# A spectral-mixing and SwiGLU kernel on one core: first batch's filter products, filter loads, weight loads and first normalisations rearranged

## The chip, the core and the metric

The kernel runs on one core of one Trainium2 chip. The metric is the device time in microseconds (us), taken as the median of 17 runs of the same program. The core has five engines that each work through their own instruction stream in order: TensorE (PE in the profile, with its weight loads as PEld), VectorE (DVE), ScalarE (ACT), GpSimd (POOL) and SyncE (SP). DMAs are issued from SP and ACT (hardware queues) and from POOL (the software queue). All matmul results land in PSUM, which GpSimd does not read in this kernel: what it multiplies is first copied out of PSUM by ScalarE.

## The reference

```python
def _attn_ref(x, filt_r, filt_i):          # x: 8 x 3008 x 256, filters: 1505 x 256
    X = np.fft.rfft(x, axis=1)
    F = (filt_r + 1j * filt_i)[None, :, :]
    return np.fft.irfft(X * F, n=x.shape[1], axis=1)

def _moe_ref(x, w_gate, w_val, w_out, rms_g):   # x: 24064 x 256, d_ff 1536
    rms = np.sqrt(np.mean(x * x, axis=-1, keepdims=True) + 1e-06)
    xn = x / rms * rms_g
    g = xn @ w_gate
    silu = g * (1.0 / (1.0 + np.exp(-g)))
    val = xn @ w_val
    return silu * val @ w_out
```

The first function filters every batch along the sequence in the frequency domain; its output, as 24,064 tokens of width 256, goes through an RMS norm and a gated feed-forward layer.

## The kernel before

**The Fourier transform** of length 3008 is split as 47 x 64. For each of the 8 batches there are these steps, and each has a small function that issues its instructions:

- `x_load(b, c)`, c = 0 to 3: the input, cast to fp16 on the way in, by two DMAs of the software queue each (L175).
- `a_unit(b, i)`, i = 0 to 11: a matmul with the table `wa` over the 64-long axis, evicted by ScalarE (L191, L193). Three units fill a chunk, which `z_store(b, c)` writes to the scratch tensor `z_tmp` in DRAM by four DMAs of the SP queue (L201). This first bounce through DRAM turns the layout.
- `t2_load(b, c)`: one chunk of eight of the 32 frequencies k2, read back from `z_tmp` (L205). A chunk needs all the stores of its batch.
- `b_unit(b, i)`, i = 0 to 15: two k2 each. Two matmuls with the table `wb` over the 47-long axis (L212) give a 128 x 512 block `psb` in PSUM; its product with the filter's real part gives `s1` (L217), with the imaginary part `s2`. In the first batch, the second product of odd units is made by GpSimd from a copy `v` that ScalarE takes out of PSUM (L221, L222); all other products are VectorE's (L217, L224).
- `bi_unit(b, i)`: four matmuls with the inverse table `wi` on `s1` and `s2` (L232), evicted by ScalarE (L237). In the first batch it comes one unit behind `b_unit`. Two units fill a chunk, which `g_store` writes to `g_tmp` (L240), the second bounce.
- `t4_load(b, c)`: four DMAs that read `g_tmp` back (L249). In the first batch half of them are issued from ScalarE's queue and half from SP's.
- `n_unit(b, m, dh)`, m = 0 to 5: the inverse over the 64-long axis, giving a tile of 512 tokens, evicted once as `y` (with the norm's gain) and once squared (L264, L271, L273). `q_unit` sums the squares by matmuls with `ones` (L281) and takes the power -1/2 on GpSimd (`rho`, L293). `rho_move` stores rho to DRAM and reads it back broadcast to all partitions (L297, L299), and `xn_unit` multiplies on GpSimd (L339). For the first tile of all, `norm_first` spreads rho by matmuls with `ident` instead (`psr`, L324) and multiplies on VectorE (L328).

**The feed-forward layer** is a list of 8 x 6 x 12 = 576 items (b, m, jt). For item i the loop issues `gv` (four matmuls, a Silu on ScalarE and a product on VectorE: L359, L363, L364), then what `plan` has for slot i, then `down` of item i-2 (four matmuls, L376). The plan is written out by hand: `at(slot, fn, ...)` puts the transform of batch b+1 between the items of batch b.

**Before that loop** stands a preamble that does the whole transform of batch 0 with little beside it. It also loads the filters: `f_load(c)`, c = 0 to 3, six software DMAs (eight for c = 0), fills partitions 0 to 63 of chunk c of `fr` and `fi` after these have been set to zero by VectorE (L450, L451, L463, L464); `f_dup(c)` copies them to partitions 64 to 127, `fr` on VectorE (L417) and `fi` on ScalarE (L418). `wi_group(g)`, g = 0 to 7, makes the table `wi` by transposing `wb` (L425 to L429). `gate(ap)` is a one-element copy on GpSimd (L436): what is behind it in GpSimd's stream is not issued until `ap` is there. `w_load(q)` loads half of the three weight matrices by three software DMAs (L441, L442).

All streams are in the order in which the program issues them (`manual_schedule`). The order around the change is, in the preamble before:

```python
        gate(st[0]["t1"][3][0:1, 5, 0:1])
        f_load(1)
        wb_load(2)
        wb_load(3)
        for c in range(3):
            t2_load(0, c)
        gate(st[0]["t2"][0][0:1, 0, 0:1])
        f_load(2)
```

and, in the plan for batch 1, `a0, b0, bs = (6, 22, 7)`: `a_unit`s from slot 6 on, `z_store`s at slots 9, 12, 15 and 18, `t2_load`s from slot 19, `b_unit`s from slot 22, seven slots for four of them.

Of the kernel before, what the change touches and what calls it, by code (L numbers as in the profile page):

```python
# [35 lines left out]
KC = 8  # L36
# [66 lines left out]
def kernel(  # L103
# [104 lines left out]
    def b_unit(b, i):  # L208
        ps = bank(0 if b else i % 2, "psb").rearrange("p (a d) -> p a d", a=2)
        for u in range(2):  # L210
            k = 2 * i + u
            nc.tensor.matmul(ps[:, u, :], wb[:, k, :], st[b]["t2"][k // KC][:, k % KC, :],  # L212
                             start=True, stop=True)
        s1 = sp.tile([P, 2, D], FP16, tag="s1", name="s1")
        s2 = sp.tile([P, 2, D], FP16, tag="s2", name="s2")
        c, r = divmod(2 * i, KC)
        nc.vector.tensor_tensor(out=s1, in0=ps, in1=fr[c][:, r:r + 2, :], op=ALU.mult)  # L217
        if b == 0 and i % 2:
            v = yp.tile([P, 2, 512], FP32, tag="y", name="v")
            v = v[:, 0, :].rearrange("p (a d) -> p a d", a=2)  # L220
            nc.scalar.activation(out=v, in_=ps, func=AXT.Copy)  # L221
            nc.gpsimd.tensor_tensor(out=s2, in0=v, in1=fi[c][:, r:r + 2, :], op=ALU.mult)  # L222
        else:
            nc.vector.tensor_tensor(out=s2, in0=ps, in1=fi[c][:, r:r + 2, :], op=ALU.mult)  # L224
        st[b]["s"][i] = (s1, s2)
# [13 lines left out]
    def g_store(b, c):  # L239
        nc.sync.dma_start(g_d[b, 4 * c:4 * c + 4, :, :].rearrange("k p d -> p k d"),  # L240
                          st[b]["t3"].pop(c))

    def t4_load(b, c):
        t = t4p.tile([P, XC, D], FP16, tag="t4", name="t4")
        for h in range(2):
            for ri in range(2):
                p0 = h * 64 + ri * 32
                r0 = ri * SL + h * H + c * XC
                (nc.scalar if b == 0 and h else nc.sync).dma_start(t[p0:p0 + 32, :, :],  # L249
                                                                   g_d[b, :, r0:r0 + XC, :])  # L250
        st[b]["t4"][c] = t
# [51 lines left out]
    def norm_first():  # L303
# [11 lines left out]
        st[0]["sq"][0] = sq  # L315
        q_unit(0, 0)
        rho = st[0]["u"].pop(0)
# [3 lines left out]
        ps = bank(1, "psr")  # L321
# [7 lines left out]
        st[0]["xn"][0] = xn  # L329
# [103 lines left out]
    def gate(ap):  # L433

        g = up.tile([1, 1], FP32, tag="gate", name="gate")
        nc.gpsimd.tensor_copy(out=g, in_=ap)  # L436

    def w_load(q):
        cols = ts(q, DFF // 2)
        for src, dst in ((moe_w_gate, wg), (moe_w_val, wv)):  # L440
            nc.gpsimd.dma_start(dst[:, :, cols], src.rearrange("(dt p) j -> p dt j", p=P)[:, :, cols])  # L441
        nc.gpsimd.dma_start(wo[:, ts(q, JT // 2), :],  # L442
                            moe_w_out.rearrange("(jt p) d -> p jt d", p=P)[:, ts(q, JT // 2), :])

    def wb_load(c):
        nc.sync.dma_start(wb[:, c * KC:(c + 1) * KC, :], wb_d[:, c * KC:(c + 1) * KC, :])

    with tc.manual_schedule():
        nc.vector.memset(mhalf, -0.5)
        nc.vector.memset(fr[0][0:HALF], 0.0)  # L450
        nc.vector.memset(fi[0][0:HALF], 0.0)  # L451
# [4 lines left out]
        f_load(0)  # L456
# [3 lines left out]
        wb_load(1)  # L460
        for c in range(NC):
            if c:
                nc.vector.memset(fr[c][0:HALF], 0.0)  # L463
                nc.vector.memset(fi[c][0:HALF], 0.0)  # L464
            for i in range(3):
                a_unit(0, 3 * c + i)
            z_store(0, c)
        nc.vector.memset(ones, 1.0)
        gate(st[0]["t1"][3][0:1, 5, 0:1])
        f_load(1)  # L470
        wb_load(2)
        wb_load(3)
        for c in range(3):
            t2_load(0, c)
        gate(st[0]["t2"][0][0:1, 0, 0:1])
        f_load(2)
# [4 lines left out]
        for g in range(4):  # L481
            wi_group(g)
        f_dup(0)
        for g in range(4, 8):
            wi_group(g)
        for i in range(17):
            if i < 16:
                b_unit(0, i)
            if i == 1:
                f_load(3)  # L490
            if i == 7:
                w_load(0)
            if i == 11:
                w_load(1)
            if i == 15:
                for c in range(NXC):
                    x_load(1, c)
            if i % 4 == 1 and i // 4 + 1 < NC:
                f_dup(i // 4 + 1)
            if i >= 1:  # L500
                bi_unit(0, i - 1)
                if i % 2 == 0:
                    g_store(0, i // 2 - 1)
            if i == 4:
                t2_load(0, 3)
        for c in range(NXC):
            t4_load(0, c)
        norm_first()
        n_unit(0, 1, 0)
        n_unit(0, 1, 1)  # L510
        q_unit(0, 1)
        rho_move(0, 1)
# [82 lines left out]
```

## Time and profile before

| What | us |
|---|---|
| median of 17 runs | 1018.61 (1016.1 to 1021.99) |
| the profiled execution, its time | 1018.67 |
| the profiled execution, its span from first to last instruction | 1016.9 |
| PE busy in the span | 931.9 (92%) |
| first matmul of the first batch's `b_unit` (L212) | 32.52 |
| first matmul of `norm_first` (L310) | 85.24 |
| first matmul of `gv` (L359) | 95.02 |
| PE busy in the 817 us from 200 us on | 797.2 |

The time of a run is 1.8 us longer than the span of its profile. A row of the timeline is: start, duration, engine, line, operation, output <- input, and in brackets how long the engine sat idle before it and what ended that. A row of the chain is start, length and what was at work. A row of the windows is a stretch, its length, then the busy time of each engine with its number of instructions, the granted TensorE clock, the share of the DMA engines and GB/s.

### The profile page before, as it was taken

What the parts mean: (1) busy time and instruction counts of PE and PEld (TensorE: products, weight loads), DVE (VectorE), ACT (ScalarE), POOL (GpSimd) and SP (SyncE); (2) the same over time, 40 slices, a digit from 0 to 9 for tenths busy, and PEclk for the clock granted to TensorE, in tenths of its full rate; (3) what the DMA queues carried; (4) which work ended last, traced back from release to release, by engine and by line L of the source; (5) the groups of instructions that cost most, each with busy time, mean ns of one, the idle gap of its engine ahead of it and who ended that gap; (6) DMA issues with size and microseconds to landing.
All of it is one profiled execution on the core that took longest, in us unless ns stands there. A gap on an engine that the chain in (4) does not pass through costs nothing.

```text
span 1016.9 us, 17359 instructions
## 1 busy us (share of the span) xinstructions
PE 931.9 (92%) x6279; PEld 570.0 (56%) x6279; DVE 601.0 (59%) x980; ACT 602.7 (59%) x1060; POOL 249.2 (25%) x221
## 2 busy tenths in 40 slices
PE   2444989999999999999999999999999999999997
PEld 1222556655665566655665566655665556656554
DVE  8532467645774477645775468644775467645554
ACT  4442755666655765567655765567656766566543
POOL 5460341032311232032411323031410322023200
PEclk9999999999999999999999999999999999999999
DMA  9994373435723374324724365324734353312211
GB/s 193 158 172 110 79 176 77 105 76 134 150 63 105 93 162 112 99 70 123 153 60 123 86 146 126 106 50 113 160 83 123 86 121 89 100 51 61 43 42 39
DMA packets 94565, 107.25 MB, mean 105 GB/s; under 512 B 17224, under 2 KB 69064, under 8 KB 94288
## 3 DMA queue, kind: packets, MB, share of 16 engines
q1 hardware_dynamic: 85104, 87.59, 33.3%
q0 software_dynamic: 8992, 17.77, 11.9%
q8 instruction: 49, 0.80, 0.3%
q10 hardware_dynamic: 384, 0.79, 0.3%
q14 instruction: 36, 0.29, 0.1%
HBM read 70.88 MB, written 49.90 MB: 119 GB/s over the span
## 4 chain that ended last, share of the span: by engine, by line
PE 75%; DMA 9%; ACT 5%; issue 4%; DVE 3%; POOL 2%; SPq 1%; ACTq 0%; DVEq 0%; POOLq 0%
PE po L376 22%; PE pg L359 21%; PE pv L359 20%; PE psi L232 5%; PE psb L212 3%; DMA z_tmp<-t 3%; DMA t<-z_tmp 3%; PE psn L264 2%; DMA fi<-in_filt_i_dram 2%; ACT t L193 1%; ACT sq L273 1%; SPq L201 1%; PE psa L191 1%; DVE s L217 1%; DMA g_tmp<-t 1%
## 5 line engine op out<-in xcount | busy, mean ns | idle before, releaser
L364 DVE TENSOR_TENSOR hh<-pv,sg 128x512 f16<-128x512 f32 (+1 forms) x576 | 390.8, 679 | 349.5 <-ACT sg L363 224.9
L363 ACT ACTIVATE sg<-pg 128x512 f16<-128x512 f32 (+1 forms) x576 | 340.6, 591 | 309.1 <-PE pg L359 306.7
L376 PE MATMUL po<-wo,hh 128*128 128x256 f16 (+1 forms) x2304 | 361.2, 274 | 3.1 <-DVE o L383 0.9
L359 PE MATMUL pg<-xn,wg 128*128 128x512 f16 (+1 forms) x1152 | 340.0, 377 | 0.0
L359 PE MATMUL pv<-xn,wv 128*128 128x512 f16 (+1 forms) x1152 | 338.8, 376 | 0.0
L376 PEld LDWEIGHTS <-hh 128*128 128x128 f16 (+1 forms) x2304 | 221.5, 98 | 110.7 <-issue 33.3
L339 POOL TENSOR_TENSOR xn<-y,rb 128x1024 f16<-128x1024 f32 (+1 forms) x47 | 129.6, 2758 | 310.9 <-DMA rb<-r_tmp 234.5
L359 PEld LDWEIGHTS <-wv 128*128 128x128 f16 x1152 | 113.1, 98 | 132.1 <-issue 2.1
L293 POOL TENSOR_TENSOR rho<-u,mhalf 128x4 f32<-128x4 f32 x48 | 48.7, 1015 | 367.3 <-DVE u L291 354.0
L359 PEld LDWEIGHTS <-wg 128*128 128x128 f16 x1152 | 105.6, 98 | 21.6
L232 PE MATMUL psi<-s,wi 128*128 128x256 f16 x512 | 85.4, 290 | 19.7 <-POOL s L222 13.1
L217 DVE TENSOR_TENSOR s<-psb,fr 128x512 f16<-128x512 f32 x128 | 87.3, 682 | 21.5 <-PE psb L212 21.4
L237 ACT ACTIVATE t<-psi 96x512 f16<-96x512 f32 x128 | 75.9, 593 | 38.7 <-PE psi L232 38.4
L232 PEld LDWEIGHTS <-wi 128*128 128x128 f16 x512 | 51.9, 103 | 54.3 <-issue 15.3
L224 DVE TENSOR_TENSOR s<-psb,fi 128x512 f16<-128x512 f32 x120 | 81.6, 680 | 0.0
L271 ACT ACTIVATE y<-psn,gsb 128x512 f32<-128x512 f32 (+1 forms) x94 | 64.4, 685 | 10.4 <-PE psn L264 5.3
L212 PE MATMUL psb<-t,wb 96*128 96x256 f16 x256 | 53.1, 292 | 14.3 <-DMA t<-z_tmp 13.7
L193 ACT ACTIVATE t<-psa 128x512 f16<-128x512 f32 x96 | 57.9, 612 | 11.9 <-PE psa L191 9.0
L273 ACT ACTIVATE sq<-psn 128x512 f16<-128x512 f32 (+1 forms) x94 | 55.6, 591 | 0.0
L191 PE MATMUL psa<-xc,wa 128*128 128x512 f16 x96 | 37.5, 408 | 10.8 <-DMA xc<-in_x_dram 9.5
L212 PEld LDWEIGHTS <-wb 96*128 96x128 f16 x256 | 24.9, 104 | 37.4 <-issue 16.3
L264 PEld LDWEIGHTS <-t 128*128 128x128 f16 x376 | 29.6, 100 | 21.6 <-issue 1.1
(52 smaller groups left out, 287.4 us busy)
## 6 DMA issues: line engine op xcount, KB each, us to landing
out_dram<-o SPq DMA_DIRECT2D x88, 256.0 KB, 3.7
z_tmp<-t SPq DMA_DIRECT2D x128, 96.0 KB, 2.2
t<-z_tmp SPq DMA_DIRECT2D x32, 384.0 KB, 6.0
g_tmp<-t SPq DMA_DIRECT2D x64, 192.0 KB, 2.5
rb<-r_tmp SPq DMA_DIRECT2D x47, 256.0 KB, 4.2
t<-g_tmp SPq DMA_DIRECT2D x120, 96.0 KB, 2.5
xc<-in_x_dram POOLq DMA_DIRECT2D x56, 192.0 KB, 6.2
out_dram<-o SPq DMA_DIRECT2D x8, 192.0 KB, 3.0
```

The source lines that it names most:

```text
L193: nc.scalar.activation(out=dst, in_=src, func=AXT.Copy)
L212: nc.tensor.matmul(ps[:, u, :], wb[:, k, :], st[b]["t2"][k // KC][:, k % KC, :], start=True, stop=True)
L217: nc.vector.tensor_tensor(out=s1, in0=ps, in1=fr[c][:, r:r + 2, :], op=ALU.mult)
L224: nc.vector.tensor_tensor(out=s2, in0=ps, in1=fi[c][:, r:r + 2, :], op=ALU.mult)
L232: nc.tensor.matmul(ps[:, u, :], wi[:, 2 * i + u, q, :], s12[q][:, u, :], start=(q == 0), stop=(q == 1))
L237: nc.scalar.activation(out=st[b]["t3"][c][:, 2 * r:2 * r + 2, :], in_=ps[0:KR], func=AXT.Copy)
L273: nc.scalar.activation(out=st[b]["sq"][m][:, dh, 0:w], in_=ps[:, 0:w], func=AXT.Square)
L339: nc.gpsimd.tensor_tensor(out=xv[:, :, 0:nq], in0=yv[:, :, 0:nq], in1=rv[:, 0:nq].unsqueeze(1).to_broadcast([P, 2, nq, P]), op=ALU.mult)
L359: nc.tensor.matmul(ps[:, 0:w], wt[:, dt_, ts(jt, P)], xn[:, dt_, 0:w], start=(dt_ == 0), stop=(dt_ == 1))
L363: nc.scalar.activation(out=sg[:, 0:w], in_=pg[:, 0:w], func=AXT.Silu)
L364: nc.vector.tensor_tensor(out=hh[:, 0:w], in0=pv[:, 0:w], in1=sg[:, 0:w], op=ALU.mult)
L376: nc.tensor.matmul(po[s4 // 2][0:w, s4 % 2, :], hh[:, s4 * P:s4 * P + w], wo[:, jt, :], start=(jt == 0 and s4 % 2 == 0), stop=(jt == JT - ...
```

## The change

The diff, cut to its core:

```diff
@@ b_unit
-        s1 = sp.tile([P, 2, D], FP16, tag="s1", name="s1")
-        s2 = sp.tile([P, 2, D], FP16, tag="s2", name="s2")
         c, r = divmod(2 * i, KC)
-        nc.vector.tensor_tensor(out=s1, in0=ps, in1=fr[c][:, r:r + 2, :], op=ALU.mult)
-        if b == 0 and i % 2:
+        f1, f2 = fr[c][:, r:r + 2, :], fi[c][:, r:r + 2, :]
+        if b:
+            s1 = sp.tile([P, 2, D], FP16, tag="s1", name="s1")
+            s2 = sp.tile([P, 2, D], FP16, tag="s2", name="s2")
+        else:
+            s1, s2 = (hp.tile([P, 512], FP16, tag=g, name=g).rearrange("p (a d) -> p a d", a=2)
+                      for g in ("sg", "hh"))
+        eng = nc.vector
+        if b == 0 and i % 2 and i > 4:
+            eng = nc.gpsimd
             v = yp.tile([P, 2, 512], FP32, tag="y", name="v")
             v = v[:, 0, :].rearrange("p (a d) -> p a d", a=2)
             nc.scalar.activation(out=v, in_=ps, func=AXT.Copy)
-            nc.gpsimd.tensor_tensor(out=s2, in0=v, in1=fi[c][:, r:r + 2, :], op=ALU.mult)
-        else:
-            nc.vector.tensor_tensor(out=s2, in0=ps, in1=fi[c][:, r:r + 2, :], op=ALU.mult)
+            ps = v
+        eng.tensor_tensor(out=s1, in0=ps, in1=f1, op=ALU.mult)
+        eng.tensor_tensor(out=s2, in0=ps, in1=f2, op=ALU.mult)
@@ t4_load
-                (nc.scalar if b == 0 and h else nc.sync).dma_start(t[p0:p0 + 32, :, :],
+                (nc.scalar if b == 0 and c == 0 and h else nc.sync).dma_start(t[p0:p0 + 32, :, :],
@@ norm_first, cut in two helpers that also take tile 1
+        scale_split(0)
+        scale_apply(0, 1)
+    def scale_split(m):
+        rho = st[0]["u"].pop(m)
         hl = up.tile([P, 2, 4], FP16, tag="hl", name="hl")
         nc.vector.tensor_copy(out=hl[:, 0, :], in_=rho)
         nc.vector.tensor_tensor(out=hl[:, 1, :], in0=rho, in1=hl[:, 0, :], op=ALU.subtract)
+    def scale_apply(m, bk):
+        ps = bank(bk, "psr")
...
@@ w_load: thirds in place of halves
-        cols = ts(q, DFF // 2)
+        cols = ts(q, DFF // 3)
...
@@ preamble
         for c in range(NXC):
             x_load(0, c)
-        f_load(0)
...
         for c in range(NC):
-            if c:
-                nc.vector.memset(fr[c][0:HALF], 0.0)
-                nc.vector.memset(fi[c][0:HALF], 0.0)
+            for t in (fr[c], fi[c]):
+                if c < 2 or (c == 2 and t is fr[c]):
+                    nc.vector.memset(t[0:HALF], 0.0)
+                else:
+                    nc.scalar.activation(out=t[0:HALF].rearrange("p a d -> p (a d)"),
+                                         in_=mhalf[0:HALF, 0:1].to_broadcast([HALF, KC * D]),
+                                         func=AXT.Copy, scale=0.0)
+        nc.vector.memset(ones, 1.0)
+        f_load(0)
+        for c in range(NC):
             for i in range(3):
                 a_unit(0, 3 * c + i)
             z_store(0, c)
-        nc.vector.memset(ones, 1.0)
-        gate(st[0]["t1"][3][0:1, 5, 0:1])
-        f_load(1)
-        wb_load(2)
-        wb_load(3)
+            if c == 1:
+                wb_load(2)
+                wb_load(3)
+                wi_group(0)
+                wi_group(1)
         for c in range(3):
             t2_load(0, c)
         gate(st[0]["t2"][0][0:1, 0, 0:1])
+        f_load(1)
         f_load(2)
...
-        for g in range(4):
+        for g in range(2, 8):
             wi_group(g)
         f_dup(0)
-        for g in range(4, 8):
-            wi_group(g)
-        for i in range(17):
+        for i in range(19):
             if i < 16:
                 b_unit(0, i)
-            if i == 1:
+            if i == 5:
+                t2_load(0, 3)
                 f_load(3)
-            if i == 7:
+            if i == 9:
                 w_load(0)
-            if i == 11:
-                w_load(1)
-            if i == 15:
-                for c in range(NXC):
-                    x_load(1, c)
-            if i % 4 == 1 and i // 4 + 1 < NC:
+            if i % 4 == 2 and i // 4 + 1 < NC:
                 f_dup(i // 4 + 1)
-            if i >= 1:
-                bi_unit(0, i - 1)
+            if i >= 3:
+                bi_unit(0, i - 3)
                 if i % 2 == 0:
-                    g_store(0, i // 2 - 1)
-            if i == 4:
-                t2_load(0, 3)
+                    g_store(0, i // 2 - 2)
         for c in range(NXC):
             t4_load(0, c)
+        gate(st[0]["t4"][0][0:1, 0, 0:1])
+        w_load(1)
+        w_load(2)
         norm_first()
         n_unit(0, 1, 0)
         n_unit(0, 1, 1)
-        q_unit(0, 1)
-        rho_move(0, 1)
+        for c in range(NXC):
+            x_load(1, c)
@@ plan
-        at(4, xn_unit, 0, 1)
+        at(1, q_unit, 0, 1)
+        at(3, scale_split, 1)
+        at(5, scale_apply, 1, 0)
         for m in range(2, 6):
-            norm_plan(0, m, (m - 2) * 10)
+            norm_plan(0, m, 2 + (m - 2) * 9)
-            a0, b0, bs = (6, 22, 7) if b == 1 else (0, 16, 8)
+            a0, b0, bs = (8, 24, 6) if b == 1 else (0, 16, 8)
```

In the first batch both products of a unit are now on one engine: GpSimd's for units 5, 7, 9, 11, 13 and 15, VectorE's for the others, and `s1` and `s2` have four buffers in place of three. The inverse follows three units behind in place of one. Three of the eight zero fills go to ScalarE. The second half of the table `wb` is loaded between the second and third group of first-bounce stores on SP, and two groups of `wi` are made there; the filters' chunk 1 is issued behind the gate on the first `t2_load`, so that all filter chunks stay on the software queue. Of the weights, the first third is loaded during the filter products, the other two thirds and the input of batch 1 behind a new gate on the first `t4_load`. The second token tile of batch 0 takes the matmul way of `norm_first` in place of the DRAM way. The plan of batches 0 and 1 is shifted.

More of the change, by code (lines that the diff above doesn't have):

```diff
@@ L315, in norm_first @@
         st[0]["sq"][0] = sq
+        st[0]["y"][0] = y
         q_unit(0, 0)
-        rho = st[0]["u"].pop(0)
+        scale_split(0)
+        scale_apply(0, 1)
+    def scale_split(m):
+        rho = st[0]["u"].pop(m)
         hl = up.tile([P, 2, 4], FP16, tag="hl", name="hl")
@@ L320, in norm_first @@
         nc.vector.tensor_tensor(out=hl[:, 1, :], in0=rho, in1=hl[:, 0, :], op=ALU.subtract)
-        ps = bank(1, "psr")
+        st[0]["u"][m] = hl
+    def scale_apply(m, bk):
+        hl = st[0]["u"].pop(m)
+        y = st[0]["y"].pop(m)
+        ps = bank(bk, "psr")
         for q in range(4):
@@ L328, in norm_first @@
             nc.vector.tensor_tensor(out=xn[:, dh, :], in0=ps, in1=y[:, dh, :], op=ALU.mult)
-        st[0]["xn"][0] = xn
+        st[0]["xn"][m] = xn
     def xn_unit(b, m):
@@ L438, in w_load @@
     def w_load(q):
-        cols = ts(q, DFF // 2)
+        cols = ts(q, DFF // 3)
         for src, dst in ((moe_w_gate, wg), (moe_w_val, wv)):
             nc.gpsimd.dma_start(dst[:, :, cols], src.rearrange("(dt p) j -> p dt j", p=P)[:, :, cols])
-        nc.gpsimd.dma_start(wo[:, ts(q, JT // 2), :],
-                            moe_w_out.rearrange("(jt p) d -> p jt d", p=P)[:, ts(q, JT // 2), :])
+        nc.gpsimd.dma_start(wo[:, ts(q, JT // 3), :],
+                            moe_w_out.rearrange("(jt p) d -> p jt d", p=P)[:, ts(q, JT // 3), :])
     def wb_load(c):
@@ L449 @@
         nc.vector.memset(mhalf, -0.5)
-        nc.vector.memset(fr[0][0:HALF], 0.0)
-        nc.vector.memset(fi[0][0:HALF], 0.0)
         warm = up.tile([P, 4], FP32, tag="rho", name="warm")
```

## The prediction

> **What bounds the kernel now.** I read the page's slices first, then the engines' windows by stage.
>
> ```profile
> PE   2444989999999999999999999999999999999997
> DMA  9994373435723374324724365324734353312211
> PE 75%; DMA 9%; ACT 5%; issue 4%; DVE 3%; POOL 2%; SPq 1%; ACTq 0%; DVEq 0%; POOLq 0%
> ```
> ```profile
> 36.00:71.00 35.00, 21.02 (x92) 12.88 (x92) 19.07 (x27) 18.83 (x26) 20.18 (x23) 1.00 1.01 150
> 71.00:94.00 23.00, 3.90 (x34) 2.87 (x33) 3.10 (x7) 3.16 (x6) 4.81 (x9) 1.00 0.69 155
> 104.00:120.00 16.00, 15.99 (x108) 9.47 (x106) 7.89 (x13) 13.25 (x24) 6.74 (x4) 1.00 0.30 66
> 120.00:140.00 20.00, 16.10 (x104) 9.44 (x102) 9.08 (x16) 9.78 (x17) 5.37 (x5) 0.91 0.67 158
> 200.00:1017.00 817.00, 797.18 (x5446) 487.81 (x5443) 489.69 (x817) 502.18 (x892) 184.41 (x136) 1.00 0.41 98
> ```
>
> From 95 us on TensorE has 96 to 100% of nearly every window: that part is its work, which the change leaves alone but for eight small matmuls. Time can come only from the preamble, where no engine is full, and from the window 120 to 140. The chain of waits names the pieces, the timeline the stations:
>
> ```profile
> 34.71 8.12 DMA fi<-in_filt_i_dram
> 43.73 1.28 POOL s L222
> ...
> 71.82 9.82 DMA g_tmp<-t
> 81.91 2.59 DMA t<-g_tmp
> ...
> 130.51 3.93 DMA t<-z_tmp
> ```
> ```profile
> 28.52 1.48 SPq L205 DMA_DIRECT2D t<-z_tmp  x3
> 32.54 0.18 POOL L436 CAST gate<-t 1x1 f32<-1x1 f16 x1 [12.09 <-DMA t<-z_tmp]
> 35.58 0.69 DVE L217 TENSOR_TENSOR s<-psb,fr 128x512 f16<-128x512 f32 x1
> ...
> 69.06 1.26 POOL L222 TENSOR_TENSOR s<-v,fi 128x512 f16<-128x512 f32 x1 [3.09 <-ACT v L221]
> ...
> 89.56 1.04 POOL L293 TENSOR_TENSOR rho<-u,mhalf 128x4 f32<-128x4 f32 x1 [14.75 <-DVE u L291]
> ```
>
> Stations: first chunk back at 32.5, first product 35.6, last inverse evicted 71.8, its store landed 81.7, first matmul of norm_first 85.24, first gate matmul 95.02.
>
> **Start and bounce.** Three zero fills go to ScalarE, 3 x 1.91 (the row of the same 64x2048 shape, f_dup's fi) after the 2.23 at which it is free: done near 8.2, while its first eviction stands at 8.88. Hidden; without that cover up to 5.7. VectorE is free at 12 in place of 18. f_load(1), 752 KB, leaves the bounce; at the 195 to 240 GB/s of the windows there it took about 3.8. The floor is SP's own issue: the last z store left at 21.1, the inserted wb loads cost it about 1, and the fastest landing of these stores was 4.0. So the reads start near 25.2, not 28.5, and land near 29.0 (28.5 to 30.5): -3.5. For wi, TensorE waited 11.8 for wb until 28.64, and VectorE's last wi came 6.9 later. The wb loads, now ahead of the last eight stores, leave near 15 and land (4.8 to 7.0) by 22: wi done at 29, f_dup(0) 1.2 more. First product 30.2, before 35.58.
>
> **Filters.** Here the change takes back. f_load(1) stands where f_load(2) stood, behind the gate at 32.54. That one's fourth DMA landed at 42.83, gate + 10.3. So chunk 1 is whole at 29 + 11 = 40 for fi and 38 for fr. VectorE makes units 0 to 2 (six products 0.60 apart) by 33.8 and stands before f_dup(1) until 38. ScalarE's copy runs 40 to 42, and behind it in its stream wait two evictions and unit 5's copy v, 0.6 each. GpSimd multiplies unit 5 from 43.8 to 46.4.
>
> t2_load(0,3), now at unit 5 on SP, is wanted by unit 12: 0. GpSimd then issues f_load(3), which took 3.9 (39.79 to 43.73): 50.3. Chunk 2 follows chunk 1 on the queue at the 104 GB/s of the windows 36 to 46, 7.3: whole near 47.5. Chunk 3 lands 8.1 (fi's median) to 9 after issue, about 58.7; f_dup(3) to 60.6; the eviction and unit 11's v to 61.8.
>
> **Products.** Before, a pair of units took 4.2 (GpSimd starts at 60.67 and 64.71 for instance): one GpSimd product, then matmuls, eviction and VectorE in a ring, since the inverse followed one unit behind. Three behind opens the ring; a pair then costs what its busiest engine needs: GpSimd 2 x 1.27 = 2.54, VectorE 2 x 0.60 = 1.2, TensorE 12 x 0.213 = 2.6, ScalarE 1.8. [...] VectorE alone would need 4 x 0.60 = 2.4 a pair plus 1.2 per f_dup[...]. I keep 2.54. Units 11, 13, 15: 61.8 + 7.6 = 69.4, bound from below by GpSimd's own chain without the wait on chunk 3: 46.4 + 3.9 + 2.54 x 2 + 2.4 (weights) + 7.6 = 65.4. f_dup(2) and f_dup(3) lie beside GpSimd's products. [...] The row says 1.67 in place of 1.27 beside a copy: 2 x 0.4, mostly ahead of the wait on chunk 3. I take 0. From GpSimd's last end to the last store took 70.32 to 71.82, 1.5. The last g store leaves at 70.7 (67 to 73): -1.1.
>
> **Second bounce.** This is the largest term. That store took 9.82 while half of the weights (1.15 MB) and x(1) (1.54 MB) were on the DMA engines (windows 62 to 80: mostly 190 to 236 GB/s). Now only a third of the weights comes before it, issued near 56 and landed by 66; the rest waits behind the gate on t4. I price the store at the 2.5 of its row in the page, the read at 3.1 (page 2.5, second of two DMAs a queue 0.6): norm_first at 70.7 + 2.5 + 0.1 + 3.1 = 76.4, before 85.24: **-8.8**.
>
> **First normalisations.** Before, 9.78 to the first gate matmul. ScalarE issued eight DMAs until 87.3, so its square came 1.3 late; now it issues two. But behind the new gate GpSimd has, in this order, six weight DMAs (4.5 to 4.8), rho(0,0), the eight DMAs of x(1) and rho(0,1): rho(0,0) starts at +4.9, before at +4.3: 0.6 later. q_unit(0,1), which stood before gv and waited for ScalarE, goes to slot 1: -1.7. First gate matmul at +8.7: **-1.1**. Issuing x(1) behind it, GpSimd lets at most eight of its DMAs be open (the issue at 43.12 waited 0.56 for the one eight earlier), so the last x waits until the weights have landed, +13.5 (1.57 MB, and 1.18 MB of t4 reads, at about 210 GB/s), and rho(0,1) comes at +15; scale_split wants it in slot 3, +16.5. A cover of 1.5: cost 0 (0 to 3). jt 4 wants the second third at +16, landed near +9; slot 8 wants x at +20, landed at +16.
>
> **Loop.** Tile 1 gives up rho_move and xn_unit: two DMAs on SP and 2.86 of GpSimd, neither on TensorE's path: 0. psr for it: 8 matmuls of 128 columns, 0.43. Units of batch 1 every 1.5 slots in place of 1.75: window 140 to 160 lost 0.8 that way; I add 0.7 (0 to 1.5). The stall: SP stood behind rho_move(0,3) at slot 15 (its read waited 3.6 for the store), the last z stores left until 128.5, the read landed 3.93 later. TensorE then ran at half pace from 134.6 to 137.6, 1.5 more: 5.5 in all. Now rho_move is in slot 16 and b_unit in 24, eight slots apart, not seven, so the stores are bound by their own evictions as in later batches. Those waited 7.8 in six batches, 1.3 each, none over 1.9 and with no slow matmuls behind. I take 1.3: **-4.2** (-5.5 to 0).
>
> **Sum** against the profiled execution, 1018.67 (span 1016.9 and 1.8 outside): -8.8 - 1.1 + 0.4 + 0.7 - 4.2 = -13.0, so 1005.7. The median of the runs, 1018.61, stands at the same place; I say 1005.5.
>
> **Rivals.** *Filters come faster.* With chunk 1 alone behind the gate its landing needs less than 11, and GpSimd's chain decides: store at 66.9, 3.8 less: 1001.7. For it: units then wait for nothing else. Against it: the windows 36 to 46 show only about 104 GB/s with the DMA engines full.
> *The wait only moves.* Chunk 3 lands later, the store leaves at 73 (+2.3), and SP is again late in the loop, with the slow clock (+4.2): 1012.
> *Slower: GpSimd's stream at the gate.* Rho(0,0) is queued behind six weight DMAs of 1.57 MB, where three weight DMAs at most were seen open at once. If the queue can't hold them, GpSimd stands until they land: rho at +14 in place of +5, rho(0,1) behind x(1) at +24 or more with VectorE's products behind it, some 7 more. 9 + 7 = 16 against the 13.0 gained: 1018.7 + 3 = 1021.7. It decides once that wait passes 13. Against it: both w_loads were issued in 2.4 each without a wait.
> *It doesn't do what it says:* chunk 1 behind the gate costs the products what the bounce saves, and the last g store, still held by other traffic, lands at 81 as now; the loop gains nothing: 1017 to 1019.
>
> **How the numbers follow.** Forecast 0.57 (1002 to 1009), faster filters 0.17, the wait moved 0.19, GpSimd's stream 0.04, nothing 0.03. What can be told from no change is 0.2%, 2 us. Faster: 0.57 + 0.17 + 0.19 = 0.93; within: 0.03; slower: 0.04. The range takes both neighbours in, with 2.7 below the faster one for the lower ends of the DMA terms: 999 to 1012.5.
>
> **What would show it.** Right: first products near 30, VectorE idle until about 38 before f_dup(1), GpSimd with two 1.27 products a pair, g store landed within 3, norm_first near 76, gv near 85, psb's wait in batch 1 under 2 with no slow matmuls. Wrong: z stores still landing at 28, a long idle of GpSimd among the six weight issues, hl waiting for rho in slot 3, or g store still taking 8.

## The result and the profile after

| | before | after |
|---|---|---|
| median, us | 1018.81 (47 runs) | 1009.56 (1008.51 to 1010.24, 8 runs) |
| after / before | | 0.9907, interval 0.9895 to 0.9919 |
| span of the profiled execution | 1016.9 | 1007.3 |
| first `norm_first` matmul | 85.24 | 73.70 |
| first gate matmul | 95.02 | 80.53 |
| PE busy share from 200 us to the end | 97.6% | 97.2% |

The change gains 9.3 us, where 13.0 were forecast for the profiled execution. The time lies in the range, but two errors of opposite sign are behind it. That shows in the page's slices and the windows of the changed kernel (same stretches as before, the last one to this kernel's own end; lines moved, L212 is still `psb`, L375 is the gate matmul, L392 the one of `down`):

```profile
PE   3448899998999999998999999999999989999997
PEclk8568999999999999999999999999999999999999
DMA  8969663236541473424632474335724353312111
PE 76%; DMA 10%; ACT 5%; DVE 3%; issue 3%; POOL 1%; SPq 1%; ACTq 0%; DVEq 0%; POOLq 0%
```
```profile
36.00:71.00 35.00, 15.80 (x76) 9.67 (x75) 14.33 (x17) 17.71 (x25) 23.60 (x24) 0.60 0.70 125
71.00:94.00 23.00, 16.91 (x129) 10.58 (x130) 10.15 (x22) 10.80 (x20) 12.12 (x19) 0.75 1.05 205
120.00:140.00 20.00, 15.06 (x97) 9.63 (x98) 11.62 (x19) 8.91 (x16) 5.67 (x6) 0.91 0.80 168
200.00:1007.30 807.30, 784.99 (x5346) 480.93 (x5345) 483.10 (x804) 494.27 (x877) 179.64 (x134) 1.00 0.41 98
```

The second window is the gain: TensorE works 16.9 of 23 us where it worked 3.9. The last two are what the forecast didn't have. From 120 to 140 us TensorE is no busier than before (15.06 against 16.10), and from 200 us on, where it should have been left alone, it is idle for 22.3 us (807.3 less 784.99) where it was idle for 19.7. (The clock column can't be compared ahead of 100 us: the record of the kernel before begins at 99.9, and its 1.00 there stands beside matmuls of 0.213, the same pace as here under 0.60.)

The chain (start, length, what was at work) and the timeline (start, duration, engine, line, operation, idle before it) name the stations:

```profile
29.80 8.28 DMA fi<-in_filt_i_dram
...
55.94 1.92 ACT fi L434
...
67.67 2.28 DMA g_tmp<-t
70.15 2.53 DMA t<-g_tmp
...
119.48 3.93 DMA t<-z_tmp
```
```profile
23.41 1.48 SPq L205 DMA_DIRECT2D t<-z_tmp  x3
...
27.21 0.18 POOL L452 CAST gate<-t 1x1 f32<-1x1 f16 x1 [12.51 <-DMA t<-z_tmp]
28.66 0.69 DVE L229 TENSOR_TENSOR sg<-psb,fr 128x512 f16<-128x512 f32 x1
36.09 1.29 DVE L433 COPY fr<-fr 64x2048 f32<-64x2048 f32 x1 [3.75 <-DMA fr<-in_filt_r_dram]
...
73.70 1.01 PE L316 MATMUL psn<-wai,t 128*128 128x128 f16 x8 [6.69 <-DMA t<-g_tmp]
77.26 1.10 POOL L299 TENSOR_TENSOR rho<-u,mhalf 128x4 f32<-128x4 f32 x1
```

The reader sees the first chunk back at 27.2 (32.5 before), the first product at 28.7 (35.6), VectorE then 3.75 idle in front of chunk 1 of the filters, the last `g_store` leaving at 67.7 (71.8) and landing in 2.28 in place of 9.82.

Where the gain goes afterwards is read by setting the same item's product (`hh`, VectorE) against itself, after minus before:

| item | 0 | 12 | 27 | 72 | 96 to 144 | 240 | 456 to 564 |
|---|---|---|---|---|---|---|---|
| difference, us | -13.95 | -16.0 | -14.2 | -13.9 | -12.1 | -10.3 | -9.6 |

The change is 16 ahead by item 12 and gives some 6.4 of it back in steps: about 2 around batch 1's first bounce, 2 during the transform of batch 2, 1.5 in that of batch 4, 1.2 in that of batch 7. (From item 72 to the end that is 4.2, which is about the 2.6 more of idle time, and a stretch of 3.4 us in batch 2 in which matmuls ran at half pace, 0.21 in place of 0.11 for 256 columns, which costs about 1.7.)

### The profile page after: what moved, and what is told of

It is laid out like the page before. It is cut to its first block, busy times and chain, and to the rows that moved or that the text cites. A ratio compares the mean times of both kernels' runs of the same rounds, so it can differ in the third digit from the quotient of the medians.

```text
span 1007.3 us, 17371 instructions
## 1 busy us (share of the span) xinstructions
PE 929.7 (92%) x6287; PEld 569.3 (57%) x6287; DVE 596.1 (59%) x977; ACT 605.9 (60%) x1061; POOL 254.2 (25%) x227
## 4 chain that ended last, share of the span: by engine, by line
PE 76%; DMA 10%; ACT 5%; DVE 3%; issue 3%; POOL 1%; SPq 1%; ACTq 0%; DVEq 0%; POOLq 0%
PE po L392 23%; PE pg L375 21%; PE pv L375 20%; PE psi L238 5%; DMA z_tmp<-t 3%; DMA t<-z_tmp 3%; PE psb L212 3%; DMA fi<-in_filt_i_dram 2%; PE psn L270 2%; ACT t L193 1%; ACT sq L279 1%; PE psa L191 1%; SPq L201 1%; DVE o L399 1%; PE psq L287 1%
## 5 line engine op out<-in xcount | busy, mean ns | idle before, releaser
L392 PE MATMUL po<-wo,hh 128*128 128x256 f16 (+1 forms) x2304 | 361.9, 274 | 3.6 <-DVE o L399 1.4
L375 PE MATMUL pg<-xn,wg 128*128 128x512 f16 (+1 forms) x1152 | 339.9, 377 | 0.0
L375 PE MATMUL pv<-xn,wv 128*128 128x512 f16 (+1 forms) x1152 | 338.9, 376 | 0.0
L392 PEld LDWEIGHTS <-hh 128*128 128x128 f16 (+1 forms) x2304 | 221.6, 98 | 113.4 <-issue 35.1
L355 POOL TENSOR_TENSOR xn<-y,rb 128x1024 f16<-128x1024 f32 (+1 forms) x46 | 126.8, 2757 | 324.8 <-DMA rb<-r_tmp 259.6
L375 PEld LDWEIGHTS <-wv 128*128 128x128 f16 x1152 | 113.0, 98 | 132.0 <-issue 1.9
L299 POOL TENSOR_TENSOR rho<-u,mhalf 128x4 f32<-128x4 f32 x48 | 48.8, 1016 | 335.3 <-DVE u L297 322.2
L375 PEld LDWEIGHTS <-wg 128*128 128x128 f16 x1152 | 105.8, 98 | 22.4 <-issue 0.6
L229 DVE TENSOR_TENSOR s<-psb,fr 128x512 f16<-128x512 f32 x112 | 76.2, 681 | 11.5 <-PE psb L212 11.5
L230 DVE TENSOR_TENSOR s<-psb,fi 128x512 f16<-128x512 f32 x112 | 76.2, 680 | 0.0
L212 PE MATMUL psb<-t,wb 96*128 96x256 f16 x256 | 52.6, 292 | 19.6 <-DMA t<-z_tmp 18.9
L277 ACT ACTIVATE y<-psn,gsb 128x512 f32<-128x512 f32 (+1 forms) x94 | 64.3, 684 | 10.7 <-PE psn L270 5.6
L238 PE MATMUL psi<-s,wi 128*128 128x256 f16 x448 | 67.3, 273 | 2.8 <-DVE s L230 2.8
L212 PEld LDWEIGHTS <-wb 96*128 96x128 f16 x256 | 25.0, 105 | 41.4 <-issue 17.4
```

The costliest lines, as they stand in the source:

```text
L229: eng.tensor_tensor(out=s1, in0=ps, in1=f1, op=ALU.mult)
L230: eng.tensor_tensor(out=s2, in0=ps, in1=f2, op=ALU.mult)
L238: nc.tensor.matmul(ps[:, u, :], wi[:, 2 * i + u, q, :], s12[q][:, u, :], start=(q == 0), stop=(q == 1))
L355: nc.gpsimd.tensor_tensor(out=xv[:, :, 0:nq], in0=yv[:, :, 0:nq], in1=rv[:, 0:nq].unsqueeze(1).to_broadcast([P, 2, nq, P]), op=ALU.mult)
L375: nc.tensor.matmul(ps[:, 0:w], wt[:, dt_, ts(jt, P)], xn[:, dt_, 0:w], start=(dt_ == 0), stop=(dt_ == 1))
L392: nc.tensor.matmul(po[s4 // 2][0:w, s4 % 2, :], hh[:, s4 * P:s4 * P + w], wo[:, jt, :], start=(jt == 0 and s4 % 2 == 0), stop=(jt == JT - ...
```

## The experiments

Each edit is made to the changed kernel; ratios are to the kernel before, beside it on the same chip. The questions: why is batch 1's wait still there and why do later batches now lose time (`e1_x2_late`, `e2_rho3_late`, `e7_b_later` to `e10_best`), and which part of the change carries the gain (`e3_all_vector` to `e6_one_behind`, `e11_split_unit`, `e12_tile1_back`).

My theory for the wait came from SP's and GpSimd's streams in the changed kernel:

```profile
104.89 2.07 SPq L411 DMA_DIRECT2D out_dram<-o  x2
107.06 0.60 SPq L303 DMA_DIRECT2D r_tmp<-rho  x1
113.29 0.34 SPq L305 DMA_DIRECT2D rb<-r_tmp  x1
113.72 3.65 SPq L201 DMA_DIRECT2D z_tmp<-t  x8
119.48 1.47 SPq L205 DMA_DIRECT2D t<-z_tmp  x3
```
```profile
105.91 1.13 POOL L175 DMA_DIRECT2D xc<-in_x_dram  x2
```

and in those of the kernel before:

```profile
120.21 0.55 SPq L297 DMA_DIRECT2D r_tmp<-rho  x1
124.43 0.34 SPq L299 DMA_DIRECT2D rb<-r_tmp  x1
```
```profile
130.77 1.15 POOL L175 DMA_DIRECT2D xc<-in_x_dram  x2
```

The last eight z stores of batch 1 stand on SP behind `rho_move(0,3)`'s read (L305), which waits for rho's own store to land: 6.2 us here, 4.2 before. All eight then leave back to back in 3.65, so it isn't their own evictions that hold them. New is the row of GpSimd: since `xn_unit(0,3)` moved to slot 21, the first input load of batch 2 (slot 20) comes ahead of it in GpSimd's stream and leaves at 105.91, just before rho's store; before, it left at 130.77, after the stall.

**`e1_x2_late`**, batch 2's input two slots later:

```diff
-                    at(t + 20 + 4 * c, x_load, b + 1, c)
+                    at(t + (22 if b == 1 else 20) + 4 * c, x_load, b + 1, c)
```


> Only the first input DMAs of batch 2 move, from slot 20 to slot 22, so that on GpSimd they stand behind xn_unit(0,3) again as in the kernel before. Theory A (GpSimd ran ahead and these DMAs, together with the output store, delayed the landing of the small rho store behind which SP's last z stores wait: 6.2 us in place of 3.6): the landing falls to about 3.6, TensorE's wait for the first chunk of batch 1 falls from 4.9 to 2 or less, no matmuls at half pace behind it, and the median falls by 3 to 5 us from 1009.6, to about 1005.5. Rival B (the order on SP alone makes the wait; the input DMAs are innocent): the wait stays 4 to 5 and the median within 1 us of 1009.6.

Measured: 1003.73 (ratio 0.986, 0.9845 to 0.9875), span 1002.0: 5.8 below the changed kernel, where 3 to 5 were expected. SP's stream and PE's wait in this run:

```profile
107.80 0.54 SPq L303 DMA_DIRECT2D r_tmp<-rho  x1
110.74 0.34 SPq L305 DMA_DIRECT2D rb<-r_tmp  x1
111.17 3.70 SPq L201 DMA_DIRECT2D z_tmp<-t  x8
116.85 1.47 SPq L205 DMA_DIRECT2D t<-z_tmp  x3
```
```profile
PE psb L212 <- DMA t<-z_tmp: 1.1, 1, 1.1
```

Rho's store lands in 2.9 and everything behind it moves up; the wait shrinks from 4.9 to 1.1 and no half-paced matmuls follow.

**`e2_rho3_late`**, `rho_move` and `xn_unit` of (0,3) eight slots later, so that no wait stands ahead of the z stores:

```diff
+            late = 8 if (b, m) == (0, 3) else 0
-            at(s0 + 5, rho_move, b, m)
-            at(s0 + 10, xn_unit, b, m)
+            at(s0 + 5 + late, rho_move, b, m)
+            at(s0 + 10 + late, xn_unit, b, m)
```


> Only rho_move and xn_unit of tile 3 of batch 0 move, eight slots later (24 and 29), so that no z store of batch 1 stands behind a wait for the rho store on SP; GpSimd still issues batch 2's first input early. Theory A and rival B both give a wait under 2 us at the first chunk of batch 1 and a median of 1004 to 1006, since SP's order is in both the place of the wait. If the wait stays at 4 or more, the z stores themselves land late and SP's order is not the place: median about 1009.

Measured: 1004.63 (0.987, 0.9854 to 0.9889), span 1000.6, PE's wait 0.7. Two different edits take the same 5 to 6 us away, so the place is SP's order and the occasion is the early input load.

**`e3_all_vector`**, all first-batch products on VectorE:

```diff
-        if b == 0 and i % 2 and i > 4:
+        if False:
```


> In the first batch VectorE makes all products of all units; GpSimd makes none and ScalarE no copy v. Theory C (the stage is paced by the landing of filter chunk 3 and by GpSimd's stream, in which its products stand between the filter issues): chunk 3 is issued as soon as chunk 2, near 34, and lands near 50, VectorE needs 2.4 us for a pair; the last g store leaves at 60 to 63 in place of 67.7 and the median falls by 4 to 6. Rival D ([...] sharing the products is the gain): VectorE becomes the bound, the last g store leaves at 68 or later, median 1009.6 or more.

Measured: 1005.01 (0.9868, 0.9853 to 0.9883), 4.5 below the changed kernel, first gate matmul 3.0 earlier (77.5). The last `g_store` leaves at 64.7, not in the expected 60 to 63. GpSimd's stream is free sooner: the first DMA of `f_load(3)` leaves at 40.05, not behind unit 5's products at 45.80:

```profile
40.05 0.54 POOL L422 DMA_DIRECT2D fr<-in_filt_r_dram  x1 [0.19 <-issue]
```

But that isn't what set the end. The later issues wait for DMAs still open (1.00 ahead of the one at 42.11, 1.25 ahead of those at 45.63), and the last part of chunk 3 lands only 0.9 sooner (55.0 against 55.9), not near 50 as expected. The chain of this run goes elsewhere:

```profile
49.73 8.79 DMA g_tmp<-t
...
58.62 0.60 ACT t L243
...
64.69 2.27 DMA g_tmp<-t
```

The first third of the weights now leaves at 46.8 in place of 54.7, a `g_store` beside it takes 8.79, and ScalarE's eviction stands until 58.6 for the buffer. What the edit saves lies behind chunk 3's copy. In the changed kernel unit 11's copy `v` stands behind `f_dup(3)` in ScalarE's stream (58.36), and three GpSimd pairs follow it, from 59.09 to 66.5. Here VectorE makes unit 11 ahead of the end of that copy (55.08), and its last product ends at 63.2.

**`e4_f1_early`**, the gate on `t1` and `f_load(1)` back ahead of the reads:

```diff
+        gate(st[0]["t1"][3][0:1, 5, 0:1])
+        f_load(1)
         for c in range(3):
             t2_load(0, c)
         gate(st[0]["t2"][0][0:1, 0, 0:1])
-        f_load(1)
```


> Filter chunk 1 goes back into the first bounce, behind the old gate on ScalarE's last eviction, and all else stays changed. Theory C (the landing of the filters paces the products): the first chunk is back at about 30.5 in place of 27.2, but unit 5's copy no longer waits for chunk 1 and chunk 2 lands near 41 in place of 45; the last g store leaves at 62 to 65 in place of 67.7, the median falls by 3 to 5. Rival E (the 3 to 4 us saved in the bounce are the gain of this edit): the last g store leaves at 69 to 71, median 1011 to 1013.

Measured: 1007.37 (0.9887, 0.9867 to 0.9907), about 2 below the changed kernel, with overlapping intervals; first gate matmul 78.8, last `g_store` at 66.0 where 62 to 65 was expected. First products come later (34.2 against 28.7), units no longer wait for chunk 1, and GpSimd's first product is only 1.5 earlier (41.86): the `wi` table, read on SP behind the z reads, came late. So the early bounce is worth less than having chunk 1, but neither decides much.

**`e5_traffic_back`**, weights and x(1) between the units again:

```diff
-            if i == 9:
-                w_load(0)
+            if i in (9, 11, 13):
+                w_load((i - 9) // 2)
+            if i == 15:
+                for c in range(NXC):
+                    x_load(1, c)
...
-        gate(st[0]["t4"][0][0:1, 0, 0:1])
-        w_load(1)
-        w_load(2)
```


> All three weight loads (units 9, 11, 13) and the input of batch 1 (unit 15) go back in front of the second bounce, the gate on the first t4 read is gone. Theory (the last g store took 9.8 because of that traffic, the largest term of the prediction): the store lands 7 to 10 after it leaves in place of 2.3, and it leaves 2 to 4 later since GpSimd issues 2.4 more per weight load between its products; first gate matmul 7 to 10 later than 80.5, less 1 that rho no longer waits; median 1015 to 1018. Rival (the store waited for its own queue, not for the traffic): it lands in 3 to 4 and the median is 1010 to 1012.

Measured: 1020.91 (1.0027, 1.0013 to 1.004): the whole gain is gone, and 3 more than expected. SP's stream, last `g_store` and then the reads behind it:

```profile
60.14 14.29 SPq L246 DMA_DIRECT2D g_tmp<-t  x5
84.13 5.99 SPq L255 DMA_DIRECT2D t<-g_tmp  x13
```

The last store leaves at 74.1 and lands 9.8 later; without the traffic it takes 2.28. It also leaves 6.5 later, where 2 to 4 were expected: the six more weight issues between GpSimd's products push its last pair back by 4.5, and the first of the three pairs begins 1.7 later.

**`e6_one_behind`**, the inverse one unit behind again:

```diff
-            if i >= 3:
-                bi_unit(0, i - 3)
+            if i >= 1:
+                bi_unit(0, i - 1)
```


> The inverse follows one unit behind again, with both products of a unit still on one engine. Theory (the ring of product, matmul, eviction set the pace of the stage before): a pair costs GpSimd's 2.54 plus the ring's rest, 4 us or more; after chunk 3's copy at 57.9 the three last GpSimd units take 12 in place of 7.4, the last g store leaves 4 to 6 later, median 1014 to 1016. Rival (the filters' landing paces the stage and the lag is idle): within 1 us of 1009.6.

Measured: 1015.77 (0.9974, 0.9963 to 0.9985), as expected; the last `g_store` leaves 6.4 later (74.0). GpSimd's stream shows the ring:

```profile
60.76 1.30 POOL L229 TENSOR_TENSOR sg<-v,fr 128x512 f16<-128x512 f32 x1
...
65.40 1.26 POOL L229 TENSOR_TENSOR sg<-v,fr 128x512 f16<-128x512 f32 x1 [2.12 <-issue]
...
70.03 1.26 POOL L229 TENSOR_TENSOR sg<-v,fr 128x512 f16<-128x512 f32 x1 [2.13 <-PE psi L238]
```

A pair starts every 4.63; three behind, 2.45 (59.09, 61.55, 63.99).

**`e7_b_later` and `e8_all_three`**, batch 1's `b_unit`s two slots later, those of the later batches two slots later and seven slots apart; the z reads go along. `e8_all_three` adds the edits of `e1_x2_late` and `e3_all_vector`.

```diff
-            a0, b0, bs = (8, 24, 6) if b == 1 else (0, 16, 8)
+            a0, b0, bs = (8, 26, 6) if b == 1 else (0, 18, 7)
```


> Only the plan of batches 1 to 7 moves: b_unit starts at slot 26 in batch 1 and 18 in the later ones (two slots later), with four units in six and seven slots. Theory F (what the loop lost, 5 us against the kernel before, are waits of TensorE for the first chunk of a batch, 4.9 and 9.3 in all, and the half-paced 3.4 us that some of them draw after them): two slots, 2.9 us, cover all later batches' waits and most of batch 1's; nothing at half pace from 85 us on; median 997 to 1001. Rival G (the waits move to the second bounce, since the last g store then stands close to its reading at slot 54): waits for t of g_tmp appear and the median is within 3 us of 1009.6.

> Three edits on the changed kernel together: all first-batch products on VectorE, batch 2's first input two slots later, b_unit two slots later in all batches. If the gains of the single edits (4.5, 5.8, and that of the third) are separate places, except that the second and third share batch 1's wait: 1009.6 - 4.5 - 5 - 6 = 994, range 991 to 998. If the third only moves waits: about 999 to 1000.

Measured: 1042.01 (1.0224, 1.0207 to 1.0241) and 1036.43 (1.0184, 1.0166 to 1.0202). Both missed by some 40 us, on the other side. PE's waits from 220 us on and SP's stream in batch 2 of `e7_b_later`:

```profile
PE psb L212 <- DMA t<-z_tmp: 21.8, 6, 3.9
PE psb L212 <- ACT t L243: 4.1, 6, 0.7
PE po L392 <- DVE o L399: 3.6, 6, 0.6
PE psb L212 <- ACT sq L279: 3.3, 6, 0.6
PE psb L212 <- DVE s L230: 2.9, 12, 0.4
```
```profile
225.54 0.34 SPq L305 DMA_DIRECT2D rb<-r_tmp  x1
225.98 2.17 SPq L411 DMA_DIRECT2D out_dram<-o  x2
228.33 2.59 SPq L205 DMA_DIRECT2D t<-z_tmp  x3
```

I had moved the reads together with their users, and two slots later the reads fall behind `rho_move` and the output store on SP, so `psb` waits 3.6 a batch where it waited 1.6, and a half-paced stretch follows in each of the six batches. The other four rows, 13.9 us together, are waits for ScalarE and VectorE that neither the changed kernel nor `e9_b_later_reads_kept` has there. The latter keeps eight slots for four units, so the seven-slot spacing is the likely cause of them; no run has the one edit without the other.

**`e9_b_later_reads_kept`**, the users later, the first three reads where they were:

```diff
-            a0, b0, bs = (8, 24, 6) if b == 1 else (0, 16, 8)
+            a0, b0, bs = (8, 26, 6) if b == 1 else (0, 18, 8)
...
-                at(t + b0 - 3 + c if c < 3 else t + b0 + 8, t2_load, b, c)
+                at(t + b0 - 5 + c if c < 3 else t + b0 + 8, t2_load, b, c)
```


> As the earlier run with b_unit two slots later, but the first three reads of a batch keep the slots of the changed kernel (21 to 23 and 13 to 15) and the later batches keep eight slots for four units. Theory H (in that run the reads themselves, moved to slots 15 to 17, had come to stand behind rho_move at slot 14 on SP, and lost there what the later b_unit gave): waits for the first chunk vanish from batch 2 on (9.3 in all, now under 1) and in batch 1 fall from 4.9 to about 2; no half-paced windows in the loop; median 996 to 1000. Rival I (b_unit two slots later is itself what cost 32, by the second bounce or by VectorE and ScalarE being crowded): median 1015 or more.

Measured: 993.75 (0.9749, 0.9732 to 0.9766), 15.8 below the changed kernel and better than expected. Everything that PE waited for on buffers from 220 us on:

```profile
PE psi L238 <- DVE s L230: 2.8, 6, 0.5
PE psa L191 <- ACT t L193: 1.1, 1, 1.1
PE po L392 <- ACT o L397: 0.2, 1, 0.2
```

The row of `psb` waiting for `z_tmp`, 9.3 in six batches in the changed kernel, is gone. In batch 1 a wait of 2.0 is left, with half-paced matmuls behind it.

**`e10_best`**: the edits of `e9_b_later_reads_kept`, `e3_all_vector` and `e1_x2_late` together.

> The last run's plan, with all first-batch products on VectorE and batch 2's first input two slots later. By theory H and the single gains (4.5 for the products, 5.8 for the input, of which the plan takes over most in batch 1): 992 to 996. By rival I: no gain over 1000.

Measured: 989.23 (0.9707, 0.9692 to 0.9723), span 987.8, below both kernels and better than expected. There is no wait of `psb` for `z_tmp` and no half-paced matmul from 80 us on; from 200 us to the end PE is busy 776.0 of 787.8, or 98.5%.

**`e11_split_unit`**: of units 5, 7 and so on, only the imaginary product goes to GpSimd, the real one stays on VectorE.

```diff
+        nc.vector.tensor_tensor(out=s1, in0=ps, in1=f1, op=ALU.mult)
         eng = nc.vector
...
-        eng.tensor_tensor(out=s1, in0=ps, in1=f1, op=ALU.mult)
```


> Of the units 5, 7 to 15 only the second product is GpSimd's, as in the kernel before, with the inverse three behind and all else changed. Theory C (GpSimd's own stream paces the last third of the stage): GpSimd needs 1.27 a pair, VectorE 1.8, ScalarE 1.8; after chunk 3's copy the last three pairs take 2.6 (TensorE) to 3 each as on VectorE alone, but f_load(3) leaves 1.3 earlier: the last g store leaves at 64.5 to 66 in place of 67.7, median 1005.5 to 1008. Rival (a unit's two products should not be split, as the change holds): 67.7 or later, 1009.6 or more.

Measured: 1008.02 (0.9891, 0.9874 to 0.9907); its interval overlaps the changed kernel's. The t4 read leaves at 69.4 in place of 70.2: 0.7 sooner, where 2 to 3 were expected. Halving GpSimd's share doesn't pay; removing it does (`e3_all_vector`), since even one product on GpSimd needs the copy `v`: unit 11's still stands behind `f_dup(3)` (58.52, in the changed kernel 58.36), and unit 5's still holds `f_load(3)` back to 45.7.

**`e12_tile1_back`**: tile 1's sum and `rho_move` ahead of the loop again, `xn_unit` in slot 4, and half of all t4 reads on ScalarE's queue.

```diff
-                (nc.scalar if b == 0 and c == 0 and h else nc.sync)
+                (nc.scalar if b == 0 and h else nc.sync)
...
         n_unit(0, 1, 1)
+        q_unit(0, 1)
+        rho_move(0, 1)
...
-        at(1, q_unit, 0, 1)
-        at(3, scale_split, 1)
-        at(5, scale_apply, 1, 0)
+        at(4, xn_unit, 0, 1)
```


> The normalisations alone go back: tile 1 of batch 0 again takes q_unit and rho_move ahead of the loop and xn_unit in slot 4, and ScalarE again issues half of all t4 reads. Theory (the prediction's two terms): the first square on ScalarE comes 1.3 later, the first gate matmul waits 1.7 more for q_unit, so it stands at 10 from norm_first's first matmul in place of 6.8; rho(0,1), behind the input of batch 1 on GpSimd, reaches tile 1's xn by slot 12 or makes TensorE wait there: median 1012 to 1016. Rival (rho on GpSimd, behind six weight loads, is the bound in either order): the first gate matmul comes less than 1 later, median within 1.5 of 1009.6.

Measured: 1007.88 (0.9904, 0.9884 to 0.9923). The first gate matmul comes 10.7 after `norm_first` in place of 6.8, as the theory had it:

```profile
85.40 1.01 PE L375 MATMUL pg<-xn,wg 128*128 128x512 f16 x2
```

By item 72 this kernel is 9.1 ahead of before, the changed kernel 13.9. Yet its median is not worse, for its later batches lose nothing (9.0 ahead in batch 2, 10.2 at the end): `psb` waits 7.2 in six batches, no half-paced matmuls follow, and the wait of `psa` is missing. The expected 1012 to 1016 missed. Why its wait of 2.01 in batch 2 drew no half pace, and why its other waits are shorter, stays open.

## Why the forecast held, and where it failed

| term of the sum | forecast | measured |
|---|---|---|
| `norm_first` earlier | -8.8 | -11.5 |
| from there to the first gate matmul | -1.1 | -3.0 |
| first slots of the loop (to item 12) | +0.4 | -1.5 |
| batch 1's stall (items 12 to 27) | -4.2 | +1.8 |
| batch 1's units closer together (items 27 to 72) | +0.7 | +0.3 |
| later batches | 0 | +4.2 |
| sum | -13.0 | -9.7 (spans: -9.6) |

That the time fell into the range is in part luck. Up to item 12 the change brings 16.0 where the sum had 9.5, and behind it the loop gives 6.3 back where the sum had a gain of 3.5: misses of 6.5 and 9.8 that nearly cancel. The measured 1009.56 is nearer to the rival *the wait only moves* (1012) than to the forecast of 1005.5.

**Start and bounce: right.** First product at 28.7, forecast 30.2; the reads left at 23.4, not 25.2.

**Filters: right in mechanism and nearly in size.** VectorE stood idle until 36.1 (forecast 38), `fi` of chunk 1 came at 39.7 (40), GpSimd's first product at 43.4 (43.8), `f_load(3)` left 45.8 to 49.8 (50.3). Chunk 3 then landed 6.65 after its last issue and not 8.1 to 9: this is the term that was mis-sized, by 2.8 up to the start of the copy, and so the last `g_store` left at 67.7 and not at 70.7 (69.4 + 1.5 in the sum is 70.9, a slip of 0.2). The price of a landing came from rows in heavier traffic: the DMA engines' share is 0.93 to 0.96 from 40 to 52 us before, and 0.66 to 0.70 from 46 to 56 us here.

**Products.** The opened ring is shown by `e6_one_behind` (4.63 to 2.45 a pair; worth 6.2 in all). The step from "VectorE alone would need 4 x 0.60 = 2.4 a pair plus 1.2 per f_dup" to keeping GpSimd's products was wrong: I took VectorE alone for no faster, and `e3_all_vector` is 4.5 faster. GpSimd's product takes about twice as long (1.26 to 0.68 in the rows), but that doesn't explain the gain: 2.54 against 2.4 a pair is nothing. I had compared products a pair and not what they wait for. The way to GpSimd leads over ScalarE's copy `v`, and unit 11's stands behind `f_dup(3)`; that wait was in my own sum for GpSimd (61.8), but I did not take it out for VectorE. The price of 0 for the copies beside products held: GpSimd's products stayed at 1.26, and VectorE's copies took 1.83 and 2.08 in place of some 1.25.

**Second bounce: right.** 2.28 for the store (forecast 2.5) and 6.03 from its leaving to `norm_first` (5.7, before 13.4). `e5_traffic_back` confirms the mechanism: with the traffic back the store takes 9.8. That run loses the whole gain, but 6.5 of its loss is that the store also leaves later. Taken back one at a time, the traffic costs 11.4 and the lag of the inverse (`e6_one_behind`) 6.2, while taking back the normalisations loses nothing at the end, and taking back the place of filter chunk 1 or GpSimd's products gains (some 2 and 4.5). The lag and the clear second bounce carry the change.

**First normalisations: right in kind, too small.** Rho(0,0) came 3.6 behind `norm_first`, not 4.9: the gate reads only the first DMA's part of `t4` and passed at 72.7, a microsecond ahead of the matmul, so the six weight issues lay beside it but for the last 0.8 (VectorE's `u` was ready at 76.5, rho started at 77.3). Gate matmul +6.8, forecast +8.7. The rival of GpSimd's stream at the gate did not happen: the six left back to back from 72.86 to 77.28. In the first slots TensorE reached its full pace 1.9 us behind the first gate matmul (82.39), before 4.9 (99.87): 3.0 less at half pace are worth 1.5, about the unforeseen gain there. As forecast, x(1) issues waited for open weight DMAs (0.4 to 1.9 each), and rho(0,1) held VectorE by 1.3 in slots 3 to 5.

**Batch 1's stall: wrong.** The failed step is "the stores are bound by their own evictions as in later batches". I counted the slots between `rho_move(0,3)` and `b_unit`, but not what the one-slot shift does to GpSimd's stream: batch 2's first `x_load` passed ahead of `xn_unit(0,3)` and its transfer met rho's store, which SP waits for. TensorE waited 4.9 us with half-paced matmuls behind, where I had 1.3 and none. `e1_x2_late` and `e2_rho3_late` show this from both sides: 5.8 and 4.9 in all, and from item 12 to item 72 they gain 3.1 and 3.5 on the kernel before, which is what the forecast had for this stretch (4.2 less 0.7). The rival *the wait only moves* had the place and the slow clock right, but put it down to late stores of the preamble, which were early.

**Later batches: not in the forecast.** Their waits were in the trace before (7.8 in six) with no slow matmuls behind; now they are 9.3. The three later steps of the item table have three rows: in batch 2 a wait of 2.02 (1.89 before), now with half-paced matmuls behind; at 456 us a wait of `psa` for ScalarE's `t` of 1.5, ScalarE standing for a z store to land; at 814 us 2.56 in place of 1.32. The change edits no step of these batches: they have narrow margins of their own, and why the last two waits came out longer was not tested. That the margin of the reads is real time is shown by `e9_b_later_reads_kept`, which removes the `psb` waits. Its profiled execution is 13.8 shorter than the changed kernel's, 1.4 of it ahead of item 72 and 12.4 behind. The waits of `psb` (9.3), the slow stretch of batch 2 (1.7) and what is less of `psa` (0.8) make 11.8 of the 12.4.

## What to carry to other kernels

When a step is moved by even one slot, list each in-order stream it stands in and what now passes ahead of it; here an input load on GpSimd's stream delayed a tiny store, for which SP waited with eight stores and TensorE behind it. Keep the small store that a queue must wait for clear of bulk transfers (6.2 to its landing beside an input load here, 2.9 without), and move a reader away from its load rather than both together: reads kept in place and eight slots for four units gave 994 us here, reads moved along and seven slots 1042. Compare engines by what the work waits for on its way to them and by what their stream carries, DMA issues included, not by the cost of the operation alone.

## What the runs showed of the hardware beyond the forecast

- **The same wait sometimes drew half pace and sometimes didn't: its length alone doesn't tell which.** A 256-column matmul takes about 0.11 at full pace and 0.21 in the slow stretches, of which the changed kernel's loop has two of 3.41 us each (from 123.35 and from 232.58). Of the waits of `psb` for `z_tmp` in the loop, over all the runs, none up to 1.93 us had slow matmuls behind; from 1.96 to 3.26 it went both ways (2.02 in the changed kernel and 2.04 in `e9_b_later_reads_kept`: slow; 2.01 in `e12_tile1_back`, 2.04 and 2.49 in `e2_rho3_late`, 2.56 in the changed kernel, 3.26 in `e8_all_three`: not); all longer ones had them. The stretches around the wait of 2.02 in the changed kernel, and around the 3.26 of `e8_all_three`:

```profile
229.17:232.58 3.41, 1.39 (x10) 1.00 0.45 116
232.58:235.99 3.41, 3.41 (x17) 0.50 0.36 42
...
591.27:594.68 3.41, 1.84 (x17) 1.00 0.89 252
594.69:598.10 3.41, 1.73 (x12) 1.00 1.19 228
598.10:601.51 3.41, 3.41 (x32) 1.00 0.16 29
```

(Behind the comma stands PE's busy time, behind the bracket the granted clock.) In the first, TensorE is idle for 2.02 of the 3.41 us ahead of the slow stretch; in the second its idle time lies over two stretches of that length, 1.57 and 1.68, and the clock stays at 1.00. So the wait of 1.89 in batch 2 before had full pace behind it, and 0.13 us more (2.02 now) came with a slow stretch that cost 1.7. What decides between the two was not shown.
- **A small store landed later beside an input load in flight.** Rho's store of a few KB, with an output store just ahead of it, took 2.9 (`e1_x2_late`), 3.2 (`e10_best`) and 4.2 (before) with no input load in flight, and 6.2 (changed) and 5.4 (`e9_b_later_reads_kept`) with one. Over the rho stores of these five runs and `e2_rho3_late` the median is 1.4 for the 203 that left without an input load in flight and 2.4 for the 74 that left beside one. A `g_store` took 2.28 alone and 9.8 beside weights and input of the software queue.
